# One product per two heads for the token scores of y, one layout for keys and tokens, fewer loads and new order tables in a linear-attention kernel

## The chip, the cores and the metric

The kernel runs on one core of one Trainium2 chip. The metric is device time in microseconds (us), the median of three runs. All data are float32. The engines are named as in the profile: PE (TensorE: matmuls; PEld its weight loads), DVE (VectorE), ACT (ScalarE), POOL (GpSimd) and SP, which only issues the loads and stores (DMAs).

## The reference

There are 4 batches and 8 heads (32 pairs), 768 tokens and 40 channels per head. The first half is a recurrence over tokens in each pair, the second a mixture of experts with soft slots over all 3072 tokens.

```python
for t in range(S):                                   # S = 768, D = 40
    y[t]  = r[t] @ state                             # state: D x D, zero at first
    Sa    = state @ a[t]
    state = state * w[t] - outer(Sa, b[t]) + outer(v[t], k[t])
x = y as 3072 x 320
logits = x @ phi                                     # 32 slots
slots  = softmax(logits over tokens).T @ x
out    = softmax(logits over slots) @ experts(slots) # 8 experts, 320 -> 1024 -> 320
```

## The kernel before, in words

**Stages.** The 768 tokens are cut into 12 stages `st` of 64 tokens, a stage into two halves `q` of 32. Heads stand in three groups `u` of 3, 3 and 2, so that a group is 120, 120 or 80 partitions (head x channel). In a stage the kernel forms running products of `w` (`scan_s`, `scan_c`, two scans on DVE), scales `k` and `b` by them (`scan_k`), spreads `a` into a block-diagonal matrix (`bd_mult`), and forms token-by-token matrices on PE (`lgram`, `gram`, `gram_0`). `kbtok`, `ctok_of`, `y_sd` and `y_ut` are PE transposes with a copy behind each.

**Solves.** Two stages together need the inverse of 1024 small triangular matrices, 32 x 32: the solve `ss` (0 to 5) for the stages 2ss and 2ss+1. `solve_in` transposes the matrices (one 128x1024 transpose on DVE, a copy on ACT), then `solve_step` 1 to 30 run one behind the other, each a multiply and an add over i x (31-i) elements (60 instructions, 30 to 240 elements wide, each needing the one before), then `solve_out` transposes back and `pairs` copies the result into the one buffer `tbs` that the chain reads. Solve 0 has a shorter form (`solve_half`, `solve_join`). A step may stand on DVE or on POOL (`nc.both`); copies may stand on DVE or ACT (`nc.either`).

**Chain.** For each half, `chain_g` gathers what state and earlier tokens give, `chain_u` multiplies by the solved matrices and writes the 32 new u tokens, and `chain_s` forms the state for the next stage. `vu` holds v and u tokens of a stage as 128 rows, `kbks` the k and b tokens in the same order of rows.

**y.** `y_p` forms, for each pair, the 128 x 64 matrix P = (v and u tokens) x (r), masks it into `ppb` on DVE, and `y_y` multiplies P by `kbks` and adds state times r. `vud` holds v and u with channels on partitions, `rds` holds r so: the heads of a pair of heads lie on partitions 0 to 39 and 64 to 103. A y_p call covers 4 heads of all 4 batches: two 32-row halves of tokens x two partition ranges x 8, which is 32 matmuls of 40 rows, 64 columns and 64 moving columns, into two PSUM banks that fill together.

**Slots and experts.** `slots_a` to `slots_e` run for every second stage; from stage 8 on the expert weights (13 MB) are loaded into buffers that stages no longer need. At the end the experts and the output products run.

**Order.** The Python code only records operations. Four tables of numbers set what is built: `ORDER` the sequence of all operations (and so of each engine), `PICK` the engine of each operation that may stand on two, `BANK` the PSUM bank of each, `PACED` the earlier load for which a load waits. An engine runs its operations strictly in its sequence. Every record of the profile has line 1178, the last line that records, so rows are told apart by tile and shape: `ps` is PSUM, `wt` and `mem` are SBUF (numbers after `wt_` differ by buffer, wt_72 is the solve's), `cs_t` the constants.

Of the kernel before, what the change touches and what calls it, by code (L numbers as in the profile page):

```python
# [14 lines left out]
MEM = 9400  # L15

B, H, S, D = 4, 8, 768, 40
# [95 lines left out]
class Engine:  # L113
# [12 lines left out]
    "Cu0203070904100005010F060I0H0G0K0J0E0R0S0A0B0C0V0U0Z0Y0W0X0a0b0h0c0d1d0f0l0e0m0N0L0M0Q1V0O0k0g1a1-1z212O1+2N1j1k"  # L126
    "221b1Z0T0i0j0n0o0s0z0u3N1u3K0t0y0p0q0r081P1X1v1q1r0w1f0+0-1l241m1o1t262511122A2C2Z2a2m2b2c2j13140x1i2B2F1g1h0v1c"
    "151628292o2p2n272G1718191A2R0D2T2P2Q0P1n1s2d2e1B1C2x331p2h1D1E1F1G2-1H1I2f2i3D2+3Z1J1K2H2g4S4v1L1M2y1N1O1Q1R2z36"
    "2E2W1S2X2I2l3738393C2J2K2Y3135346T7C5G5v2D2k322w2v4O4Q4M4q3S3o3T3r3A3V4u3B3E5H5u4Y4d5i5tAj631y1Y1e3P3Q3W3X3Y4E3R"
    "2r2L1T2t232U2u3b3p2V4k2q3F3O303j4-3H3L3a4C3U3q3I3J5U3d3e3f3g3c3k4g204h1U4e2M4j1W4i1w6V3h3i3l3m4D4F4I4G4J4H4P3n3s"  # L130
    "4W4b3t3u4f4X4c3v3w3x3y4R4T3z3+4U4n6i3-4041424344454647485N5I5L494A601x6Z6U6a2s565C4K4L3G3M4N4a4l4r4t5l4V4Z6g5O5P"
    "6K5j714m4p4o4w59585B5A575J5k6A4y516O6P6x6w5D5E5M4s4x4z6S7u4B4+50525354555T6G6N5V5W6W6c5y5X5Y6-705Z5a5b5c5R5r5m5q"
    "5n5p5o5d5e696X7B5f5g6m6n6o6p6H6J6q6r6Q6R6s6t6u6v727D7G7H7I686L6Y7f7z6B6E6I78797765675z64615+666b5-2S8B747A6C6D6F"
    "6l6k6j916d88629B9D999G7U7V5K5S5h5x757E7F7N5s5w7M7Q7d9I7L7c5F5Q6M6y6z7R7b7X7Z7a7S7T7i7t767O7g7w737JA0937K7j7y6h6+"
    "7P7h7v8C8R8-6f8H7x8h7e7l9V7+808182837-847m8T9F8F8f7W7Y8S8g8m7k9E8W8i8j8+8d8Y8D856e8789978A8G86APAT9A9+8a8k8l8E95"
    "949890AD92BQBfB1B6BRBS8b8c8e8z8n8p9CAFBcBdBo8V8ZAHA7AAAcAGAd8U8X8oA19JA5ANBp9H9z9w9x9v9yAMALBOBqC1CAA4ACA2AyB0B5"
    "AIAJDoCUCoDqAEAKAW9-A8A9BHBI7n7o7p7q7r7s8I8J8K8LDtDuEb8M8N8O8P8Q8q8r8sAhAxAm96AO8t8u8v8w8x8y9K9LA3A-9M9N9O9P9Q9R"
    "9S9TAXAaAbAYAZAtAv9U9WABA+Be9X9Y9Z9aEhEoEqGY9b9c9d9e9f9g9h9i9j9kB9BA9l9mA6AV9n9o9p9q9r9s9t9uBlBtBuBsBmAwAzB8EREc"
    "IXB-C0BDBEBPIYJHKnNjBMBUBLASARAiAeAqArAfApAQAoCZB3BKBNBYBZAUCcAkCdAnCaAlEOEPBbBnB4BFAsAuBTBVBWBkBrBgB2B7BhAgBGC+"
    "BiBvB+C3BBBCBJCBCHCGCFCECfC-CCCLC2C7BxByBwC9CzEdBjCICJBXBaC4CvDzCDCTCWCVE0CgCmBzC5DgChD4D2CiD1DnD3DxEKF6CyEGEMEZ"  # L140
    "DrDyD+CKCeE9EBECETEVEWCbE5CYCXE6E1E8E3D-FaFRE+FAEAEFEHE7FcE2FdE4FeFYENEQF7FKELEXD0DpCxD5EIESEUFEEyF1GEDsDvFGEkEn"
    "GzFFFHCwDwEDEEEJEgEuGIEfEtEwExF2EvFJFCFDF8GGGPEYElEsFBEiEjFyFzH4GkGlGvH2F3F4F5EaEmEeEpErC6C8CMCNCOCPCQCRCSCjJ0J8"
    "KACkClCnCpCqCrCsCtFnFxFkFjFhD6D7D8D9DADBDCDDEzF0DEDFDGDHDIDJDKDLF9FIFMFPFQFLFODMDNE-FZFNDODPDQDRJQJRJaJcDSDTDUDV"
    "DWDXDYDZDaDbFUFVDcDdFoG8DeDfDhDiDjDkDlDmG9GMGLGVGNFpF+F-K0JgKgMYG6G7G0G1G4KFKmNVONFwFvGHFWFXFbFlFiFuFtFTFSIHIBGi"
    "GmG2G3GCFsIgFgIhFfIFFmG5GZIzJ6GAGBGJGKGTGUGDGSGaGRFqFrGQITIUJOGFGWH7HAGcGfGgGeGsGoGqGpH3GrINItGnGyG-IvG+H5IxIuGt"
    "GuH6GdGjIKGhGxILIsICIGIJGOGwGXGbHaHBIOIPIQISH+HzIVIWKDIMIaH1H9I-J9JDH8IRJBJEJIJ1J7IZIkIDIfIpIiImIIIqIlIjJkJCJbIc"
    "IwJAIrJtIoJmJiJGInH0J5JTJUIdJ3IyJ4I+J2JMJWJZK4KHKRK-IbIeK1JSJzJyJXK8KqKsJKJNJPJJJVLNJdJhK6K7JeKEJfK2K3KzLKLOJwKM"
    "KJKOKIKPKGK9LULcLdMEMHKZKbKeJLJxJ-JYKNHCHDHEHFHGHHHIHJHKHLMQN9MXHMHNHOHPHQHRHSHTLILYJFJvJsHUHVHWHXHYHZHbHcKKKLHd"
    "HeHfHgHhHiHjHkKtKxKvKyL2L7KwHlHmJ+K5KCHnHoHpHqMxNDNNPiHrHsHtHuHvHwHxHyH-I0KWKlI1I2LRLTI3I4I5I6I7I8I9IAL3L4L9L6L5"
    "LJLXLZNYMINbMZK+LPLSLeLfQ2R8SBSCKTKSKQJjJnJrJqJpJlJuJoKBMgLDL0L8LFLGLHMAMTLxM1L-M3KVKdL1LWKULyLzKaLLLMKXKjKrKuLa"  # L150
    "LhLiM0M6M7M9M8M5M4KYKhMBMSKcKpMLMWMJMKMMLbLgMCKfKkMuMyMjMpLBKiKoLQLVOpMNN8NANBMwMvMPNKNPL+MDNONQNTNJNMNRNSNZMlMk"
    "MrMsMnMqMoMmMtO5O9NHNoNWNXNaLAN-O2O1MhMeLCLEMfMdMbMcM2N7NFNfNLNcNUNdMONCNENlNmPTPUPXNGNINnOGNeNiNpNwOFPbNrNtNvNu"
    "NsOKOOPSPZPdNxOPNqOMPjQ0Q1Q3QINkNyOHNgNhOLLjLkLlLmLnLoLpLqLrLsQOQoR3LtLuLvLwMFMGMRMUOWP3O4O8O0MVMaMzM+M-N0N1N2N3"
    "N4N5N6OZOaObOcOIOVOJOTOSOkOUOROdOeOfOgOhOiPkQEQFQrOjOlOmOnOoOrOsOtOuOvOQPEOwOxOyOzO+O-P0P1P2PLPOPPPgQQQJPDPMPNRC"
    "QHRyRlOYPFPIRKSST1TSODOEP9PAP8OBO6P7OCPmPBP4PGPHIEMiROQcQeQYOXP5PKPYPVPWPfOqP6NzO3N+Q6O7OAPcPtPJPQPaPlPyPzPrPqQG"
    "PpPeQyPvP-PwP+Q4PCPoPsQPQRQ7Q8QWQKQVQNQTQLPRQMQUQ5QDQ+Q-R5QlQnQpQAQbQ9QZQCQBQaQXQdRURNR0R1R9QgQhQjQsR4RARHR7RFRG"
    "QkQmPuQSQvR2QxQqQtRdRLRhRgRjRiRfReQiRIRkR6RJQzRERqRmRuS5SFRDRnRoQuQwRBSOSUSLRbRvS8ThSzSWSjRZS9SERsRwRxS7RaRtSwS6"
    "TFSdSJSKSRSTRRRTS2RSRYRQRPS1RXRcS0TcRrS3R+SDRpSQT9TfSMSPTdQfTXTYPnRMSASHSVSYSXPhPxRzTsR-S4SgSeSlSGSISySNSfSZSbSh"
    "SoSsT0SkSnSiSmTZUMRWUZRVTaUNTbUbTeTgTiTkTzSpSrSuSaScT2TjSqSvSxStS+S-T7T3T4T5T6TtTvU3UYT8TDTETGTITJTATBTHTNTCTOTK"
    "TLTPTQTRTTTUTVTlTmTMTrUBUCUFUHUUUVTWU7U6U4U5U8TnTpTqT+T-UKU9UQURTuTyUAUSUDULTwToTxU0U1UEUIUGUJU2UOUXUWUTUPUaVTVU"  # L160
    "VWUfUgUjUkUlUcUdUeUhUiUmUnUoUpVKUqVBUrUvUyUtUxUwUzU-U+ViV0V4V5UuV1V6V8UsV2V3V9VQVSVRVAVGVbVVVYVLVsVoVpV7VCVFVXVt"
    "VuVwVvVIVOVDVEVJVNVHVMVPVcVaVjVdVeVkVlVZVfVgVhVnVmVqVr"
)
PICK = (
    "1111111011101011111110111110111111111111101110111111111111111011110110000110111100000010111111111111111101110111"
    "1110100111101111111111011111111111111111111111111101100111011111111111111111111011111100111111110000100000111111"
    "0001011111111111101111111111111111111111111111101111111011111011010111001111101111111101111110011001110001000100"
    "0000011111111111111111110111111111111111111111111111101111101101111011110011101111111111111110111111001111111110"
    "0010111111111111111111111111111011111111111111111111111111101111110111101111100111000111001011001001111111101110"
    "0010100001001111111111111111111111111001101011111100101110100101110100111100010010101011011111001111101110110011"  # L170
    "0000001110000"
)
BANK = (
    "0124330665270356725170002715272651376477011662725022576356353677314002527664236431054353014141760614503307542036"
    "4112000525435170332747620055514236215264115760656350364577213000251211745346746053267560420137745611203447604257"
    "7463660534374045170563617055724023305471707031557670623623465312771643617171525354542056247615463136335114020744"
# [1265 lines left out]
```

## Time and profile before

| | us |
|---|---|
| median of 3 runs (404.92 to 413.21) | 405.3 |
| the profiled execution, its own time | 405.49 |
| its span, first to last instruction | 403.7 |
| PE busy | 337.1 |
| DVE busy | 295.4 |
| POOL busy | 199.4 |
| ACT busy | 189.4 |
| 16 DMA engines busy, mean | 56.6% |

The span has four stretches by what runs: the start up to the first transpose of solve 1 (57 us), five solves with the chain of stages 0 to 9 beside them (57 to 307), the last two stages with their y and slots (307 to 357), and experts and output (357 to 404). Busy time of PE includes the modelled way of each matmul through the array, so neighbours overlap. 1.8 us of the profiled time lie outside the span.

### The profile page before, as it was taken

The page shows a single profiled execution, that of the slowest core. Times are in us where ns is not written, and L with a number is a line of the kernel's source. Part 1 is how long each engine was busy: PE and PEld are TensorE (multiplying, and loading weights), DVE is VectorE, ACT ScalarE, POOL GpSimd, SP SyncE. Part 2 cuts the span into 40 slices and gives each one's busy share as a digit, 9 for nine tenths or more (in the row PEclk, how much of TensorE's full clock was granted, in tenths as well). Part 3 has the DMA queues.
Part 4 walks back from the last instruction along what each step waited for, and adds up shares of the span by engine and source line. Part 5 has one row for each costly group of instructions (what it writes and reads, how often), then busy time and mean ns, then how long its engine had stood idle before and what let it go on. Part 6 is the DMA issues. An engine that isn't in the chain of part 4 may idle for free.

```text
span 403.7 us, 18293 instructions
## 1 busy us (share of the span) xinstructions
PE 337.1 (84%) x8097; PEld 295.6 (73%) x8097; DVE 295.4 (73%) x563; ACT 189.4 (47%) x399; POOL 199.4 (49%) x280
## 2 busy tenths in 40 slices
PE   0496689988899798999769998599989899889960
PEld 0386578877798797899569988588888887633960
DVE  7999979688799778998377897478778487651160
ACT  2332546655767456756444763545143514233140
POOL 6933825888167981599824998424860000030000
PEclk9999559999699899999956999999999899989995
DMA  7994804276814734328116577467779667980066
GB/s 186 262 233 113 210 3 97 53 188 147 203 54 107 170 92 120 83 64 229 45 62 145 157 182 237 142 157 232 225 169 248 207 203 208 312 296 13 3 175 215
DMA packets 65966, 63.06 MB, mean 156 GB/s; under 512 B 35857, under 2 KB 53633, under 8 KB 65889
## 3 DMA queue, kind: packets, MB, share of 16 engines
q1 hardware_dynamic: 65889, 61.91, 56.6%
q8 instruction: 63, 1.03, 1.1%
q14 instruction: 14, 0.11, 0.1%
HBM read 57.96 MB, written 3.93 MB: 153 GB/s over the span
## 4 chain that ended last, share of the span: by engine, by line
PE 38%; POOL 31%; DVE 13%; issue 8%; DMA 4%; ACT 2%; SPq 0%; DVEq 0%; POOLq 0%; ACTq 0%
PE ps L1178 38%; POOL wt L1178 31%; DVE wt L1178 11%; DMA wt<-in_kb_dram 3%; ACT wt L1178 1%; DMA wt<-in_ww_dram 1%; ACT mem L1178 1%; DVE ps L1178 1%; DVE mem L1178 1%; DVE mid L1178 0%; SPq L1178 0%; DVE slx L1178 0%; DVE old L1178 0%; ACT mid_r L1178 0%; DMA mem<-in_rd_dram 0%
## 5 line engine op out<-in xcount | busy, mean ns | idle before, releaser
L1178 POOL TENSOR_TENSOR wt<-wt 128x234 f32<-128x234 f32 (+14 forms) x237 | 151.4, 639 | 85.9 <-DVE wt L1178 38.0
L1178 PE MATMUL ps<-wt,wt 120*32 120x96 f32 (+9 forms) x3432 | 149.8, 246 | 32.3 <-POOL wt L1178 17.3
L1178 PEld LDWEIGHTS ps<-wt,wt 120*32 120x32 f32 (+7 forms) x3432 | 134.6, 135 | 42.4 <-POOL wt L1178 17.5
L1178 ACT ACTIVATE wt<-ps 32x320 f32<-32x320 f32 (+1 forms) x129 | 55.4, 429 | 30.5 <-PE ps L1178 28.8
L1178 PE MATMUL ps<-cs_t,wt 120*128 120x120 f32 (+4 forms) x448 | 65.3, 284 | 2.5 <-DVE wt L1178 1.7
L1178 DVE TENSOR_TENSOR wt<-ps,cs_t 128x512 f32<-128x512 f32 (+2 forms) x96 | 56.8, 612 | 10.1 <-PE ps L1178 9.6
L1178 ACT COPY wt<-ps 128x320 f32<-128x320 f32 (+2 forms) x81 | 39.5, 507 | 41.4 <-PE ps L1178 38.3
L1178 PEld LDWEIGHTS ps<-cs_t,wt 120*128 120x128 f32 (+4 forms) x448 | 49.5, 148 | 7.2 <-DVE wt L1178 2.4
L1178 DVE TENSOR_TENSOR_SCAN wt<-wt,wt 120x781 f32<-120x781 f32 (+1 forms) x24 | 46.1, 1926 | 2.2 <-DMA wt<-in_ww_dram 1.6
L1178 PE MATMUL ps<-mem 64*64 64x40 f32 (+2 forms) x648 | 41.1, 253 | 5.0 <-DVE wt L1178 4.0
L1178 PE MATMUL ps<-wt,mem 64*64 64x40 f32 (+3 forms) x1072 | 40.1, 254 | 3.6 <-issue 1.7
L1178 PEld LDWEIGHTS ps<-wt,mem 64*64 64x64 f32 (+3 forms) x1072 | 36.6, 135 | 7.5 <-issue 3.3
L1178 DVE TENSOR_TENSOR wt<-wt 128x108 f32<-128x108 f32 (+19 forms) x91 | 34.3, 377 | 10.0 <-POOL wt L1178 7.6
L1178 POOL TENSOR_TENSOR wt<-wt,wt 120x768 f32<-120x768 f32 x17 | 34.4, 2033 | 9.3 <-DMA wt<-in_aa_dram 4.3
L1178 DVE STREAM_TRANSPOSE wt<-wt 128x1024 f32<-128x1024 f32 x12 | 24.8, 2068 | 18.7 <-POOL wt L1178 17.4
L1178 ACT ACTIVATE wt<-wt,bm_t 120x768 f32<-120x768 f32 (+1 forms) x35 | 29.0, 861 | 12.1 <-POOL wt L1178 4.0
L1178 PEld LDWEIGHTS ps<-mem 64*64 64x64 f32 (+2 forms) x648 | 26.8, 141 | 9.7 <-DVE wt L1178 5.0
L1178 PE MATMUL ps<-mem,wt 40*64 40x64 f32 x1536 | 29.0, 228 | 0.3 <-DVE wt L1178 0.2
L1178 PEld LDWEIGHTS ps<-mem,wt 40*64 40x64 f32 x1536 | 26.4, 142 | 2.7 <-issue 1.2
L1178 ACT COPY mem<-ps 120x480 f32<-120x480 f32 (+4 forms) x45 | 18.1, 408 | 20.6 <-PE ps L1178 11.8
L1178 DVE TENSOR_TENSOR wt<-wt,wt 120x768 f32<-120x768 f32 x20 | 23.8, 1198 | 0.2 <-DMA wt<-in_kb_dram 0.2
L1178 DVE TENSOR_TENSOR ps<-ps,wt 120x480 f32<-120x480 f32 (+1 forms) x30 | 17.8, 602 | 6.7 <-PE ps L1178 6.7
(96 smaller groups left out, 282.5 us busy)
## 6 DMA issues: line engine op xcount, KB each, us to landing
wt<-in_w_dram SPq DMA_DIRECT2D x16, 640.0 KB
wt<-in_kb_dram SPq DMA_DIRECT2D x36, 240.0 KB
wt<-in_w_dram SPq DMA_DIRECT2D x16, 512.0 KB
wt<-in_ww_dram SPq DMA_DIRECT2D x12, 366.6 KB
mem<-in_rr_dram SPq DMA_DIRECT2D x36, 120.0 KB
mem<-in_rd_dram SPq DMA_DIRECT2D x48, 80.0 KB
wt<-in_vv_dram SPq DMA_DIRECT2D x24, 160.0 KB
wt<-in_vd_dram SPq DMA_DIRECT2D x48, 80.0 KB
```

What stands on the lines that cost most here:

```text
L1178: nc.gpsimd.memset(ysb, 0.0)
```

## The change

- **P of y.** `rds` becomes 2048 columns wide, zeroed once, and holds r of the two heads of a pair beside each other in block-diagonal form. One matmul of 104 rows, 128 columns (all 64 v and 64 u tokens) and 128 moving columns gives P of two heads at once: 8 matmuls where 32 stood. Four of them fill a bank, so a call has two banks that fill one after the other; masks and their number stay.
- **Layout.** All 64 v tokens stand ahead of the 64 u tokens, and k ahead of b in the same way (`kb`, `kbks`, `vu`, `vud`, the masks). Instruction counts there stay.
- **Loads.** Per stage v comes in one load instead of two, r and v with channels on partitions in two loads instead of four each (the rows of v now 256 bytes, not 128). For the group of two heads 80 rows are loaded instead of 120 (r from the first stage, k, b and a from stage 5). 321 loads and stores become 261.
- **Buffers.** Two of three `q0s` buffers move into `wt4`; `mem` shrinks by 270 columns. POOL zeroes `rds` once, ahead of everything.
- **Tables.** ORDER, PICK, BANK and PACED are new. Of the 300 solve steps 137 stand on DVE instead of 63, 163 on POOL instead of 237; of the 71 steps of 210, 220, 238 and 240 elements on POOL 27 are left. Of the copies and small multiplications that may stand on DVE, 23 move to ACT or POOL and 8 come.

```diff
-        rds = space(1024)
+        rds = space(2048).rearrange("p (a c) -> p a c", a=2)
...
-        vud = late7[:, 0:2048].rearrange("p (x q c k t) -> p x q c k t", x=2, q=2, k=2, t=32)
+        vud = late7[:, 0:2048].rearrange("p (x c k t) -> p x c k t", x=2, c=8, k=2)
...
         def bdr_at(st):
-            for x in range(2):
-                for p in range(2):
-                    r = slice(64 * p, 64 * p + D)
-                    load(vud[r, x, :, :, 0].rearrange("p q c t -> p (q c) t"), vd[st, p, :, x].rearrange("d (c t) -> d c t", t=32))
-                    load(rds[r, 512 * x:512 * x + 512], rd[st, p, :, x])
+            for p in range(2):
+                r = slice(64 * p, 64 * p + D)
+                load(rds[r, p], rd[st, p].rearrange("d x c -> d (x c)"))
+                load(vud[r, :, :, 0].rearrange("p x c t -> p (x c) t"), vd[st, p].rearrange("d x (c t) -> d (x c) t", t=64))
...
         def vload(st):
             vu = vus.put(st)
-            for q in range(2):
-                load(vu[64 * q:64 * q + 32], vv[st, 32 * q:32 * q + 32])
+            load(vu[0:64], vv[st])
...
         def y_p(st, x):
-            g = [bank(f"ppp{st}"), bank(f"ppq{st}")]
-            nc.gather = True
             for k in range(2):
+                g = bank(f"pp{st}")
                 for b in range(B):
-                    for q in range(2):
-                        for p in range(2):
-                            r = slice(64 * p, 64 * p + D)
-                            c = 64 * (B * k + b)
-                            nc.tensor.matmul(g[p][64 * q:64 * q + 64, c:c + 64],
-                                             vud[r, x, q, B * k + b].rearrange("p k t -> p (k t)"),
-                                             rds[r, 512 * x + c:512 * x + c + 64], start=True, stop=True)
-            nc.gather = False
-            for p in range(2):
+                    c = B * k + b
+                    nc.tensor.matmul(g[:, 128 * b:128 * b + 128], vud[0:104, x, c].rearrange("p k t -> p (k t)"),
+                                     rds[0:104, :, 512 * x + 64 * c:512 * x + 64 * c + 64], start=True, stop=True)
                 t64 = lambda t: t.rearrange("p (g t) -> p g t", t=64)
-                nc.vector.tensor_tensor(t64(ppb.put(4 * st + 2 * x + p)), t64(g[p]),
+                nc.vector.tensor_tensor(t64(ppb.put(4 * st + 2 * x + k)), t64(g),
                                         mask_p.unsqueeze(1).broadcast_to([128, 8, 64]), ALU.mult)
...
 PICK = (
-    "1111111011101011111110111110111111111111101110111111111111111011110110000110111100000010111111111111111101110111"
+    "0101111010011110111111111111111111111100101111111111111111111111111111111100110011001110000011000111001111111111"
```

**On DVE, within solve 3.** The program order of DVE in before, from about the middle of the solve: `wt_72<-wt_72` are solve steps (the shape is i x width), `wt_70<-wt_70,wt_71 120x780` is a scan, `ps_62<-ps_62,wt_76` and `wt_76<-` the state (`chain_s`), `wt_77<-ps` masks of P or gram_0.

```order
L1178 TENSOR_TENSOR wt_72<-wt_72 128x9x22
L1178 MEMSET ones 128x1
L1178 TENSOR_TENSOR wt_72<-wt_72 128x210
L1178 SCALAR_TENSOR_TENSOR wt_70<-wt_70,wt_71 120x780
L1178 TENSOR_TENSOR ps_62<-ps_62,wt_76 120x480
L1178 TENSOR_TENSOR wt_77<-ps_61,cs_t 96x384
L1178 TENSOR_TENSOR wt_76<-ps_62,wt_77 120x480
```

The same place of the same solve on DVE in the changed program:

```order
L1163 TENSOR_TENSOR wt_72<-wt_72 128x220
L1163 RECIPROCAL wt_71<-wt_71 120x12
L1163 TENSOR_TENSOR wt_72<-wt_72 128x11x20
L1163 SCALAR_TENSOR_TENSOR wt_70<-wt_70,wt_71 120x780
L1163 TENSOR_TENSOR wt_72<-wt_72 128x228
L1163 TENSOR_TENSOR wt_77<-ps_66,cs_t 128x512
L1163 TENSOR_TENSOR wt_77<-ps_61,cs_t 128x512
L1163 TENSOR_TENSOR mem<-ps_63,mem 128x128
L1163 TENSOR_TENSOR wt_72<-wt_72 128x12x19
L1163 TENSOR_TENSOR wt_77<-ps_64,cs_t 128x512
```

In before the 210-wide add is the last step of solve 3 on DVE, and the scan and all behind it run while POOL does the other 40 steps; now steps of every width stand between the scan, the masks and the rest.

**On POOL, within solve 3.** POOL's program order in before, from the multiply of step 10 on:

```order
L1178 TENSOR_TENSOR wt_72<-wt_72 128x10x21
L1178 TENSOR_TENSOR wt_72<-wt_72 128x220
L1178 TENSOR_TENSOR wt_72<-wt_72 128x11x20
L1178 TENSOR_TENSOR wt_72<-wt_72 128x228
L1178 TENSOR_TENSOR wt_72<-wt_72 128x12x19
L1178 TENSOR_TENSOR wt_72<-wt_72 128x234
L1178 TENSOR_TENSOR wt_72<-wt_72 128x13x18
```

and in the changed program (`wt_73<-wt_73,wt_70` is the multiplication in `scan_c`, `wt_77<-wt_71,bm_t` a small one in `scan_s`):

```order
L1163 TENSOR_TENSOR wt_72<-wt_72 128x210
L1163 TENSOR_TENSOR wt_72<-wt_72 128x10x21
L1163 TENSOR_TENSOR wt_77<-wt_71,bm_t 120x36
L1163 TENSOR_TENSOR wt_73<-wt_73,wt_70 120x768
L1163 TENSOR_TENSOR wt_72<-wt_72 128x234
L1163 TENSOR_TENSOR wt_72<-wt_72 128x13x18
L1163 TENSOR_TENSOR wt_72<-wt_72 128x17x14
```

Steps 10 to 29 stood in one run on POOL; now POOL has two to seven steps at a time, and other work between them.

**On SP, at the start.** The first loads in before (`b` is b of the first two stages, `ww` is w, `kb` k and b):

```order
L1178 DMA wt_70<-in_ww_dram 120x782
L1178 DMA wt_74<-in_aa_dram 120x768
L1178 DMA wt_76<-in_b_dram 120x768
L1178 DMA wt_74<-in_aa_dram 120x768
L1178 DMA mem<-in_b_dram 120x768
L1178 DMA wt_70<-in_kb_dram 120x512 x4
```

and in the changed program:

```order
L1163 DMA wt_70<-in_ww_dram 120x782 x2
L1163 DMA wt_74<-in_aa_dram 120x768
L1163 DMA wt_70<-in_kb_dram 120x512
L1163 DMA wt_73<-in_aa_dram 120x256
L1163 DMA mem<-in_b_dram 120x768
L1163 DMA bm_t<-in_consts_dram 120x3
L1163 DMA wt_74<-in_aa_dram 120x768
L1163 DMA cs_t<-in_consts_dram 128x32
L1163 DMA wt_76<-in_b_dram 120x768
```

b of stage 0 (`wt_76`) was the seventh load and is now the tenth, behind a part of k that stage 1 needs and a part of a that stage 2 needs.

## Rows read from the trace of the kernel before

**Rows 1.** Page, part 1: busy us (share of the span) xinstructions.

```profile
PE 337.1 (84%) x8097; PEld 295.6 (73%) x8097; DVE 295.4 (73%) x563; ACT 189.4 (47%) x399; POOL 199.4 (49%) x280
```

**Rows 2.** Windows: from:to, length, busy PE PEld DVE ACT POOL, PEclk, DMA, GB/s.

```profile
0.00:57.00 57.00, 32.97 (x881) 29.38 (x882) 50.42 (x70) 21.44 (x36) 33.65 (x23) 0.84 0.71 178
57.00:105.00 48.00, 42.85 (x1137) 38.80 (x1136) 39.36 (x68) 29.06 (x58) 33.53 (x48) 0.96 0.51 117
105.00:157.00 52.00, 48.21 (x1178) 45.04 (x1178) 42.64 (x68) 31.46 (x64) 33.69 (x50) 0.92 0.44 114
157.00:206.00 49.00, 41.59 (x1044) 37.40 (x1040) 38.91 (x70) 28.93 (x61) 34.14 (x49) 0.96 0.39 105
206.00:262.00 56.00, 50.39 (x1191) 46.21 (x1191) 41.96 (x74) 30.76 (x66) 38.26 (x57) 0.87 0.62 167
262.00:307.00 45.00, 43.27 (x1153) 38.55 (x1150) 35.11 (x77) 18.26 (x43) 22.74 (x47) 0.98 0.73 205
307.00:357.40 50.40, 46.17 (x1125) 38.79 (x1121) 35.24 (x97) 18.04 (x48) 1.01 (x4) 0.97 0.80 238
```

**Rows 3.** Chain in order of time: start, us, what (solve 2, three of its steps).

```profile
130.40 1.98 POOL wt L1178
...
139.36 0.68 POOL wt L1178
140.10 0.60 POOL wt L1178
```

**Rows 4.** Groups by shape on POOL: xcount | busy us, mean ns | idle before.

```profile
L1178 POOL TENSOR_TENSOR wt<-wt 128x238 f32<-128x238 f32 x19 | 19.1, 1004 | 2.4 <-DVE wt L1178 1.0
L1178 POOL TENSOR_TENSOR wt<-wt 128x240 f32<-128x240 f32 x19 | 18.3, 963 | 1.5
...
L1178 POOL TENSOR_TENSOR wt<-wt 128x210 f32<-128x210 f32 x16 | 14.5, 904 | 6.3 <-DVE wt L1178 5.3
L1178 POOL TENSOR_TENSOR wt<-wt 128x220 f32<-128x220 f32 x17 | 13.8, 813 | 4.6 <-DVE wt L1178 3.4
...
L1178 POOL TENSOR_TENSOR wt<-wt 128x130 f32<-128x130 f32 x13 | 5.9, 455 | 4.5 <-DVE wt L1178 3.8
```

**Rows 5.** Groups by shape on DVE, 57 to 307 us: solve steps.

```profile
L1178 DVE TENSOR_TENSOR wt<-wt 128x130 f32<-128x130 f32 x7 | 2.1, 295 | 1.5 <-POOL wt L1178 1.2
...
L1178 DVE TENSOR_TENSOR wt<-wt 128x240 f32<-128x240 f32 x1 | 0.4, 408 | 1.6 <-POOL wt L1178 1.6
```

**Rows 6.** Groups on DVE, whole span: closing and opening transposes of solves; copies from PSUM.

```profile
L1178 DVE STREAM_TRANSPOSE wt<-wt 128x1024 f32<-128x1024 f32 x12 | 24.8, 2068 | 18.7 <-POOL wt L1178 17.4
...
L1178 DVE COPY wt<-ps 128x320 f32<-128x320 f32 (+2 forms) x27 | 13.1, 515 | 9.0 <-PE ps L1178 8.2 <-ACT mem L1178 0.8
```

**Rows 7.** Timeline of POOL and of DVE, 129 to 145 us: start, us, engine, operation, xcount.

```profile
128.92 8.85 POOL L1178 TENSOR_TENSOR wt<-wt 128x240 f32<-128x240 f32 x7
...
130.01 1.95 DVE L1178 TENSOR_TENSOR_SCAN wt<-wt,wt 120x780 f32<-120x780 f32 x1
...
137.95 7.30 POOL L1178 TENSOR_TENSOR wt<-wt 128x234 f32<-128x234 f32 x10
```

**Rows 8.** Waits of DVE, 57 to 307 us: us in total, times, longest.

```profile
DVE wt L1178 <- POOL wt L1178: 25.3, 14, 6.9
```

**Rows 9.** Timeline of PE: start, us, operation (rows x columns, moving), xrecords.

```profile
171.06 1.16 PE L1178 MATMUL ps<-mem,wt 40*64 40x64 f32 x64
172.04 0.67 PE L1178 MATMUL ps<-mem 64*64 64x40 f32 x17
...
224.95 0.65 PE L1178 MATMUL ps<-cs_t,wt 128*104 128x128 f32 x4
225.43 0.73 PE L1178 MATMUL ps<-wt,wt 128*80 128x80 f32 x8
226.00 0.74 PE L1178 MATMUL ps<-cs_t,wt 80*128 80x80 f32 x6
```

**Rows 10.** Chain in order of time at the start.

```profile
6.06 10.20 DMA wt<-in_kb_dram
```

## What the change will do to the time

> **What bounds the kernel now.** I read the busy shares first, then the windows by stretch, then the groups by shape, the chain and the waits. Over the whole span no engine is full: PE 84%, DVE 73% [rows 1]. The windows say more [rows 2]. In the five stretches from one solve's opening transpose to the next (57 to 307 us, 250 us in all) PE is busy 42.85 + 48.21 + 41.59 + 50.39 + 43.27 = 226.3 us (91%) and DVE 39.36 + 42.64 + 38.91 + 41.96 + 35.11 = 198.0 us (79%), while POOL is busy about 162 us, most of it solve steps. So three things run near their ends at once: PE's work, DVE's work, and the serial chain of 60 steps in each solve, to whose end the next two stages are tied. In the tail (307 to 357) PE alone is near full, 46.17 of 50.4 us.
>
> What do the steps cost? A step of 234 elements on POOL takes 0.60 to 0.68 us, and steps start 0.74 us apart (139.36 to 140.10) [rows 3]; ten of them fill 7.30 us [rows 7]. Just before, seven steps of the widest forms needed 8.85 us, and one of them 1.98 us: it began at 130.40, and DVE had begun a scan of 1.95 us at 130.01 [rows 3, 7]. So a POOL step is stretched while DVE runs an operation from SBUF to SBUF. In the mean the 71 widest steps on POOL are busy 19.1 + 18.3 + 14.5 + 13.8 = 65.7 us [rows 4]; at the clean 0.60 each they would take 42.6. About 23 us are stretching. DVE itself does a step of 240 elements in 0.41 us and one of 130 in 0.30 [rows 5], against 0.60 and 0.455 on POOL [rows 3, 4].
>
> DVE is idle 250 − 198 = 52 us of the loops. Of that 25.3 us are waits on POOL [rows 8], and over the whole span 17.4 us of such waits stand before the transposes of the solves [rows 6], that is, DVE had nothing else left and waited for the end of a solve. Without them 27 us remain, nearly all behind PE.
>
> **The change part by part.** *Solve steps.* 74 steps go from POOL to DVE, 44 of them of the four widest forms (71 on POOL become 27). On the chain a wide one gains 0.60 − 0.41 = 0.19 us, plus up to 0.05 for the shorter gap between steps: 44 x 0.24 = 10.6. The other 30 gain 0.455 − 0.295 = 0.16 each: 4.8. The engine changes 74 more times within the solves (42 to 116); a hand-over is not shown apart, and I bound it between 0 and the 0.07 between two POOL steps, taking half: −2.6. The chain is 12.8 us shorter. Then the 27 wide steps left on POOL carry 27/71 of the stretching, 8.8 us instead of 23: another 14.3. If the chain alone set the time, the loops would go from 250 to **223** us.
>
> DVE pays for it: 44 x 0.41 + 30 x 0.30 = 27 us more. 23 copies and small operations leave it and 8 come, 15 net at 0.5 us [rows 6] = −7.5. Six more operations run ahead of solve 1's opening transpose than before (75 for 69), which takes some 5 us out of the loops and into the start. DVE in the loops: 198 + 27 − 7.5 − 5 = **213 us**. That is 95% of 223, so the chain cannot have all of its gain. DVE is in strict order: in before the last steps of solve 3 on POOL ran with nothing of the solve queued on DVE, and a mask that waited for PE delayed no step. Now steps of every width stand behind scans, masks and copies, so each wait of DVE for PE becomes a wait of the chain. I take the loops from DVE: 213 us busy, the 27 us behind PE as they are, and waits on POOL of 5 us (before, 25.3 − 17.4 = 7.9 outside the transposes, taken lower because POOL's runs become shorter). The wait before the transposes goes, since DVE now does part of the late steps itself. Sum 245, **−5 us**. The bounds: 223 (−27, the chain alone) and DVE at its present 79%, 213/0.79 = 270 (+20).
>
> *P of y.* The tiled product is 64 records, and the next group starts 172.04 − 171.06 = 0.98 us after it [rows 9]. The new one is 8 matmuls of 128 columns, by the two records per matmul of before (64 for 32) 16 records. Eight records of 80 columns are followed after 226.00 − 225.43 = 0.57 us, 0.071 each, so 0.114 for 128 columns; four transposing records of 128 columns after 225.43 − 224.95 = 0.48, 0.12 each [rows 9]. So 16 x 0.114 = 1.83 us: **0.85 us more** each, 0.94 by the other row. There are 24, of which 20 fall in the loops: PE 226.3 + 17 = 243 of 250 us. It lies beside the solves and costs nothing there as long as PE has a pause elsewhere; with the loops at 245 that is 99% of PE, and a part of the pauses now spent behind DVE must close. The other four fall in the tail: 3.4 us on an engine that is busy 46.17 of 50.4 us. About half can be hidden in its 4.2 us of pauses: **+1.5** (0 to +3.4). The two PSUM banks now fill one after the other, so the first mask can start 0.9 us earlier; nothing waits there that long. Masks and their number stay.
>
> The Trainium skill (TensorEngine Tiling (Array Packing), Theoretical Speedup) speaks against this part: where dimensions are at most 64, tiles are said to give up to 2 times per dimension. By it the full array would take as much as four times as long, 3.9 us for 0.98, +70 us of PE over 24. The rows agree in sign but not in size, since block-diagonal r puts two heads through each pass; they give 1.9 times.
>
> *Start.* b of stage 0 moves from seventh load to tenth, and DVE has six more operations ahead of solve 1. In before, k and b are the transfer waited for at the start (6.06, 10.20 us) [rows 10], and DVE is busy 50.42 of 57 us [rows 2], so 5 us of added DVE work have 6.6 us of pauses to go into. A part will not fit: **+1.5** (0 to +5).
>
> *Loads.* 60 fewer loads and stores, behind a DMA that is not a bound (16 engines busy 39 to 80% in the windows of rows 2): **−0.5** at most. The new order of rows in `vu`, `kbks` and the masks moves no instruction and costs nothing; zeroing `rds` stands on POOL ahead of everything, under the first loads.
>
> *Sum.* Against the profiled time of 405.5 us, 0.2 above the median: −5 + 1.5 + 1.5 − 0.5 = −2.5, **403.0 us**.
>
> **The rivals.** *R1, faster: DVE fills its pauses.* If the searched order also puts each mask behind the PE work that it needs, the 27 us behind PE shrink and the loops go towards the chain's 223. For it: in 105 to 157 DVE already reached 82%. Against it: 95% on an engine that takes from PE, ACT, POOL and DMA. Midway, at 234 (DVE at 91%): 405.5 − 16 + 2.5 = **392**. It needs 89% of DVE or more to pass the 2% bound (loops under 239).
>
> *R2, slower: DVE's waits grow with its share of the chain.* DVE keeps the share of idle time it has, since a wait for PE now holds up the chain too. At its best share of today, 82%, 213 takes 260 (+10): **418**; at 79% 428. It decides below 83.4%, where the loops pass 255 and the time 413.4. For it: DVE is at 75 to 82% in all five stretches, though their other loads differ. Against it: half of today's idle time was behind POOL, and has lost its cause.
>
> *R3, slower: PE becomes the bound.* 243 us of PE work in the loops; its stretches reach 85 to 96% today. At 94.5%, between 93 and the best 96, the loops take 257 (+7): **415**. For it: 17 us come and none go. Against it: busy time is modelled and overlaps.
>
> *R4: the tiled product costs its neighbours too.* If each one emptied the array before and after, dropping 24 would give time back. The row bounds it: 16 rounds of four tiles at 0.057 (64 columns at the 0.071 for 80) are 0.91 of the 0.98, so at most 0.07 per product inside and, granting as much again on both sides, 0.2: 24 x 0.2 = 5 us of PE, about **398**, if PE is what holds. A rule of the Trainium skill on the same page (Key Properties: a change of tiling mode drains the TensorE) says that such a cost exists; no row of before shows more than this.
>
> **How the numbers follow.** The likeliest case 0.40, R1 0.29, R2 0.15, R3 0.12, R4 0.04. The first alone would range from 397 to 413, since its bounds are those of DVE's share between 83.4 and 89%. Faster by over 2% (under 397.2) is R1, and the lower half of R4 and of the first case gives it 0.04 more: 0.33. Slower (over 413.4) is R2 and R3: 0.27. The rest, 0.40, is within 2%, which is about what a measurement of this kernel can tell from no change. For 8 in 10 the range takes R1 down to 390 and R2 and R3 up to 419.
>
> **What would show it.** Right, if DVE's share in the loops lies at 84 to 89%, the loops near 49 us each, no wait on POOL over 2 us before the transposes, most wide steps at 0.41 us on DVE, and the ones left on POOL nearer 0.65 than 0.9. The new product must show 16 records and about 1.8 us to the next group; solve 1's opening transpose comes at 57 to 60 us; the tail takes 52. R1 shows as DVE over 89%, R2 as many DVE waits for PE with POOL idle behind DVE, R3 as PE over 94% in each stretch with DVE waiting for it. Wrong altogether it would be if the granted clock fell for longer than now (0.87 to 0.98 in the loops [rows 2]), since PE has no room for it.

## The result and the profile after

The changed kernel takes 388.6 us in the median (385.6 to 392.4, four runs) against 406.4 of the kernel before in the same rounds: a ratio of 0.955 (95% interval 0.946 to 0.964). Forecast were 403.0 us, 390 to 419, with "faster" at 0.33. The direction was that of the first rival (392), and the median lies 1.4 us under the range. Executions of one kernel differ by up to 4% here, the slower ones mostly at a lower mean clock, and the ratios and their intervals are of the fast ones alone.

The busy times of the page (part 1), and windows of the trace, cut where before was cut: the start up to solve 1's opening transpose, five stretches from one opening transpose to the next (the last ends with solve 5's closing one), tail, experts. The columns are those of rows 2.

```profile
PE 338.2 (88%) x6945; PEld 300.5 (78%) x6945; DVE 298.0 (78%) x622; ACT 192.0 (50%) x408; POOL 145.1 (38%) x213
```

```profile
0.00:60.11 60.11, 36.23 (x950) 32.68 (x951) 49.19 (x75) 26.41 (x50) 25.68 (x23) 0.80 0.68 180
60.11:102.82 42.71, 41.46 (x928) 38.94 (x926) 39.48 (x77) 24.15 (x48) 21.66 (x34) 1.00 0.39 93
102.82:150.03 47.21, 46.49 (x1000) 43.63 (x998) 43.15 (x78) 30.54 (x64) 25.77 (x38) 1.00 0.55 117
150.03:198.08 48.05, 47.15 (x1007) 43.84 (x1005) 44.45 (x88) 34.28 (x75) 25.52 (x37) 1.00 0.55 136
198.08:245.59 47.51, 47.09 (x1031) 44.10 (x1032) 42.10 (x88) 29.59 (x61) 23.61 (x35) 1.00 0.60 147
245.59:287.46 41.87, 40.66 (x799) 37.29 (x799) 34.59 (x82) 18.12 (x41) 19.45 (x42) 1.00 0.82 234
287.46:338.00 50.54, 46.68 (x849) 38.68 (x844) 34.12 (x97) 18.48 (x48) 3.40 (x6) 0.97 0.84 239
338.00:383.80 45.80, 32.42 (x408) 21.34 (x408) 10.93 (x41) 10.39 (x26) 0.00 (x0) 0.80 0.44 127
```

Beside rows 2: the start is 3.1 us longer, the tail and the experts are the same to half a microsecond, and all of the gain is in the loops, 227.4 us for 250. There PE is busy 222.9 us, 98%, at a granted clock of 1.00 in every stretch, where rows 2 showed 0.87 to 0.98. DVE is busy 203.8 us, 90%; POOL's busy time falls from 162 to 116. On the chain of work that ended last (page, part 4) PE's share rises from 38 to 67% of the span, and POOL's falls from 31 to 4%.

Solve steps by shape on POOL, and one on DVE (groups as in rows 4 and 5):

```profile
L1163 POOL TENSOR_TENSOR wt<-wt 128x220 f32<-128x220 f32 x10 | 9.3, 934 | 9.7 <-DVE wt L1163 9.4
...
L1163 POOL TENSOR_TENSOR wt<-wt 128x210 f32<-128x210 f32 x8 | 6.1, 760 | 3.0 <-DVE wt L1163 2.7
L1163 POOL TENSOR_TENSOR wt<-wt 128x238 f32<-128x238 f32 x5 | 5.3, 1060 | 8.0 <-DVE wt L1163 7.9
L1163 POOL TENSOR_TENSOR wt<-wt 128x240 f32<-128x240 f32 x4 | 3.9, 984 | 6.2 <-DVE wt L1163 6.2
```

```profile
L1163 DVE TENSOR_TENSOR wt<-wt 128x240 f32<-128x240 f32 x16 | 6.5, 406 | 1.1 <-POOL wt L1163 0.7
```

All steps on POOL together, before and after, and DVE's transposes of the solves after (groups of the pages, the second answering to rows 6):

```profile
L1178 POOL TENSOR_TENSOR wt<-wt 128x234 f32<-128x234 f32 (+14 forms) x237 | 151.4, 639 | 85.9 <-DVE wt L1178 38.0 <-ACT wt L1178 31.6
```

```profile
L1163 POOL TENSOR_TENSOR wt<-wt 128x30 f32<-128x30 f32 (+14 forms) x163 | 99.5, 610 | 101.8 <-DVE wt L1163 84.3
...
L1163 DVE STREAM_TRANSPOSE wt<-wt 128x1024 f32<-128x1024 f32 x12 | 25.7, 2139 | 1.2 <-POOL wt L1163 0.4
```

DVE's waits in the loops (us in total, times, longest; rows 8 of before), three of the rows:

```profile
DVE wt L1163 <- PE ps L1163: 6.4, 13, 1.2
DVE wt L1163 <- POOL wt L1163: 4.9, 11, 0.8
DVE ps L1163 <- PE ps L1163: 4.6, 7, 1.3
```

A step left on POOL is stretched as much as before, 0.76 to 1.06 us for the four widest forms (0.81 to 1.00 before), but there are 27 of them for 71. The wait for the end of a solve is gone: 0.4 us before the transposes for 17.4 [rows 6]. No wait of DVE is longer than 1.3 us.

### The profile page after: what moved, and what is told of

Same layout as the page of the kernel before. It is cut to its first block, busy times and chain, and to the rows that moved or that the text cites. A ratio compares the mean times of both kernels' runs of the same rounds, so it can differ in the third digit from the quotient of the medians.

```text
span 383.8 us, 15934 instructions
## 1 busy us (share of the span) xinstructions
PE 338.2 (88%) x6945; PEld 300.5 (78%) x6945; DVE 298.0 (78%) x622; ACT 192.0 (50%) x408; POOL 145.1 (38%) x213
## 4 chain that ended last, share of the span: by engine, by line
PE 67%; ACT 9%; DVE 8%; issue 5%; POOL 4%; DMA 3%; SPq 1%; DVEq 0%; ACTq 0%; POOLq 0%
PE ps L1163 67%; DVE wt L1163 7%; ACT wt L1163 7%; POOL wt L1163 4%; DMA mem<-in_b_dram 2%; ACT mem L1163 1%; SPq L1163 1%; DMA mem<-in_vq_dram 1%; DVE mid L1163 0%; ACT L1163 0%; ACT mid L1163 0%; DVE ps L1163 0%; DVE mem L1163 0%; DMA wt<-in_kb_dram 0%; ACT old L1163 0%
## 5 line engine op out<-in xcount | busy, mean ns | idle before, releaser
L1163 PE MATMUL ps<-wt,wt 96*32 96x40 f32 (+9 forms) x3432 | 138.9, 237 | 18.7 <-ACT wt L1163 16.6
L1163 PEld LDWEIGHTS ps<-wt,wt 120*32 120x32 f32 (+7 forms) x3432 | 126.0, 128 | 25.2 <-issue 17.6
L1163 POOL TENSOR_TENSOR wt<-wt 128x30 f32<-128x30 f32 (+14 forms) x163 | 99.5, 610 | 101.8 <-DVE wt L1163 84.3
L1163 DVE TENSOR_TENSOR wt<-ps,cs_t 128x512 f32<-128x512 f32 (+2 forms) x104 | 62.0, 618 | 7.2 <-PE ps L1163 6.3
L1163 ACT COPY wt<-ps 128x320 f32<-128x320 f32 (+2 forms) x87 | 41.7, 503 | 39.5 <-PE ps L1163 31.7
L1163 DVE TENSOR_TENSOR wt<-wt 128x234 f32<-128x234 f32 (+18 forms) x165 | 54.1, 328 | 9.3 <-POOL wt L1163 4.5
L1163 PE MATMUL ps<-mem,wt 104*128 104x128 f32 (+1 forms) x640 | 57.8, 258 | 0.3 <-DMA mem<-in_rd_dram 0.2
L1163 PEld LDWEIGHTS ps<-mem,wt 104*128 104x128 f32 (+1 forms) x640 | 53.3, 169 | 2.1 <-issue 0.6
L1163 POOL TENSOR_TENSOR wt<-wt,wt 120x768 f32<-120x768 f32 x17 | 29.8, 1770 | 26.0 <-DMA wt<-in_kb_dram 19.4
L1163 ACT COPY mem<-ps 120x480 f32<-120x480 f32 (+4 forms) x52 | 21.1, 419 | 27.6 <-PE ps L1163 26.4
L1163 PE MATMUL ps<-mem 120*64 120x120 f32 (+2 forms) x392 | 30.3, 259 | 0.0
L1163 DVE STREAM_TRANSPOSE wt<-wt 128x1024 f32<-128x1024 f32 x12 | 25.7, 2139 | 1.2 <-POOL wt L1163 0.4
L1163 ACT COPY wt<-wt 120x768 f32<-120x768 f32 (+3 forms) x19 | 16.2, 856 | 12.6 <-DVE wt L1163 11.1
```

The costliest lines, as they stand in the source:

```text
L1163: nc.vector.memset(one_f, 0.0)
```

## The experiments

The theories: A, the split of the steps shortened the chain until PE was left as the bound; B, the searched order did it, or DVE or the chain still holds the loops; C, part of the gain is the granted clock; D, the new product or the fewer loads did it. Each run has the kernel before timed beside it; a ratio is to that, and stands where the record has one. In the texts on record, A and B are the theories of that one run. Loops are again solve 1's opening transpose to solve 5's closing one: 250.3 us before, 227.4 after.

**The code under the old tables.** The changed code, with ORDER, PICK, BANK and PACED of before:

```
 ORDER = (
-    "6n0005060A011L0L0P0H0J0C020G07030B0D0E0h0R0F0T0V0b0i0p0n0f0j0N0a0e0g0l1i0u0x0v0r0O0K0Q0I0M0814180k0Y090Z0U0d0X0z"
+    "Ce0304080A0511000106020G070J0I0H0L0K0F0S0T0B0C0D0W0V0a0Z0X0Y0b0c0i0d0e1c0g0m0f0n0O0M0N0R1V0P0l0h1Z1+1y1-2M1z2L1i"
...
```

> The changed code (product of 104 rows, new layout, 261 loads) under the tables of the kernel before: old order, old engines of all steps and copies, old banks; merged loads stand where they fit beside the old ones. Theory A (the code costs PE 0.85 us per product and brings nothing by itself, since the chain of the solves holds the old order): 405 to 420 us against 405 to 416 of the kernel before on this chip. Theory D (the product or the fewer loads are what brought the gain): under 396 us.

424.1 us, ratio 1.034 (1.017 to 1.050). The loops in a window, and PE's longest waits in them:

```profile
57.36:315.91 258.55, 235.84 (x4709) 216.78 (x4709) 197.86 (x353) 137.47 (x288) 163.15 (x251) 0.95 0.53 131
```

```profile
PE ps L1169 <- DMA mem<-in_rd_dram: 10.8, 4, 5.1
```

D falls: the code without its tables costs time. PE's busy time grows by 9.5 us. But 10.8 us are waits for the merged loads of r, which land too late in this order, so the run does not price the product alone. Taken off, they would leave some 413 us, an estimate, which is still no gain.

**The split in the old order.** The kernel before, with only the characters of PICK that belong to solve steps as in the changed one (160 of 300 steps change engine, 117 of them to DVE and 43 to POOL; the 74 of the prediction is the difference):

```
 PICK = (
...
-    "1111111011101011111110111110111111111111101110111111111111111011110110000110111100000010111111111111111101110111"
+    "1111111011101011111110111110111111111111101110111111111111111011111111111110110011001010000011000111001101110111"
...
```

> The kernel before with one thing changed: each solve step stands on the engine that it has in the changed kernel (137 on DVE, 163 on POOL), in the old order. Theory A (the shorter chain of the solves brought the gain, and the order only makes room for it): most of the gain is here, 388 to 394 us. Theory B (the searched order of everything else brought it; the steps now stand behind masks and copies that wait for PE): 400 to 412 us.

485.3 us, ratio 1.185 (1.167 to 1.204): the longest of all. The profile is of the longest of its four executions, 493.9 us; the shortest took 481.2. One of three pauses of PE of about 20 us, and DVE at the same time (timelines):

```profile
142.59 1.13 PE L1178 MATMUL ps<-mem,wt 40*64 40x64 f32 x62
162.57 1.67 PE L1178 MATMUL ps<-wt,wt 120*96 120x96 f32 x9 [18.84 <-POOL wt L1178]
```

```profile
148.28 2.23 DVE L1178 TENSOR_TENSOR wt<-wt 128x238 f32<-128x238 f32 x5 [1.51 <-POOL wt L1178]
152.71 0.38 DVE L1178 TENSOR_TENSOR wt<-wt 128x210 f32<-128x210 f32 x1 [2.20 <-POOL wt L1178]
...
161.47 0.95 DVE L1178 TENSOR_TENSOR wt<-wt,wt 120x768 f32<-120x768 f32 x1
162.34 0.69 DVE L1178 TENSOR_TENSOR wt<-ps,cs_t 128x512 f32<-128x512 f32 x1
```

From 142 to 161 us DVE runs nothing but solve steps and waits for POOL's steps between them. The scaling of k and the mask of P, for which PE waits, stand behind the last step in DVE's order. (The row names POOL, whose own last step ends at the same time, 162.5.) The same split that the changed kernel has is ruinous where the steps stand next to each other: a wait for POOL on DVE then holds up everything, and there are 80.6 us of them:

```profile
DVE wt L1178 <- POOL wt L1178: 80.6, 52, 5.1
```

Theory A, as I stated it, falls.

**The old split in the new order.** The changed kernel with the steps' engines of before, by the same edit the other way:

```
 PICK = (
...
-    "0101111010011110111111111111111111111100101111111111111111111111111111111100110011001110000011000111001111111111"
+    "0101111010011110111111111111111111111100101111111111111111111111110110000100111100000110111111111111111111111111"
...
```

> The changed kernel with one thing undone: each solve step stands on the engine that it had in the kernel before (63 on DVE, 237 on POOL), in the new order. Theory A (the split of the steps): the chains grow by 13 us and the stretching on POOL returns, 400 to 410 us. Theory B (the order of the rest): at most 393 us.

424.9 us, ratio 1.040 (1.030 to 1.050): 36 us over the changed kernel. Loops, and DVE's waits in them:

```profile
61.34:326.55 265.21, 240.64 (x4759) 223.56 (x4759) 181.50 (x337) 137.69 (x285) 155.88 (x259) 0.92 0.49 124
```

```profile
DVE wt L1163 <- POOL wt L1163: 31.7, 14, 5.2
DVE wt L1163 <- PE ps L1163: 30.3, 24, 4.8
```

Here PE's work is that of the changed kernel, and still PE is busy 240.6 us for 222.9: about 41 of the 265 us ran at half clock (a mean of 0.92), and none of the changed kernel's loops did.

So B in its plain form falls too. The fair comparison is with the other run of the new code under the old split: with the old order that took a ratio of 1.034, with the new order it takes 1.040, so the new order alone gains nothing. DVE has 22 us less to do than in the changed kernel and still waits 31.7 us for POOL, and 42.1 us for PE over all rows. Split and order bring the gain only together. The new code with the new split in the old order was not run; that case is shown on the old code alone, by the run ahead of this one.

**Dummy matmuls in PE's pauses of before** (a table that is empty in both kernels):

```
 FILLS = (
-    ""
+    "7RBFAB9BG+PFJuH7"
```

> The kernel before with dummy matmuls of 128 columns (11, 9, 25 and 17 of them) ahead of the four operations at which PE pauses for 2.8, 2.3, 6.3 and 4.2 us (99.9, 134.4, 198.7 and 256.0 us) and after which the granted clock falls to half for 7, 3, 17 and 3 us. Theory C (part of the gain of the change is the clock: without the pauses PE keeps 2.4 GHz): the 30 us at half clock go, worth up to 15 us of PE's work: 392 to 398 us. Against it (what PE does at half clock there is hidden behind the solve's chain, or the clock falls for another reason): 403 to 408 us.

418.5 us, ratio 1.022 (1.010 to 1.035): no gain, but the run is half a test. The first place did what it should. PE in before, and here (windows):

```profile
103.40:110.20 6.80, 6.80 (x78) 6.45 (x68) 5.49 (x5) 5.37 (x12) 0.00 (x0) 0.50 0.84 208
```

```profile
102.00:110.00 8.00, 7.37 (x220) 6.80 (x212) 7.98 (x9) 7.15 (x15) 0.99 (x4) 1.00 0.99 224
```

With the pause filled, the fall of the clock behind it is gone. At the second place PE paused for 1.0 and 0.5 us ahead of the dummies, and the clock fell all the same. The last two groups waited themselves, as it seems for the PSUM bank in which I had put them (line 379 is theirs):

```profile
PE ps L379 <- DVE wt L1178: 5.8, 1, 5.8
PE ps L379 <- ACT wt L1178: 3.5, 1, 3.5
```

so they filled nothing and came on top. In all, the loops ran about 33 us at half clock, as many as before (windows of half a microsecond). That pauses and clock belong together is shown at one place; what the clock alone is worth in this kernel stays open.

**The tiled product in the new order.** P as it was formed before, in 10 stages, then in the three (3, 8, 10) where nothing else has to move:

```
+            for c in range(2 * B):
+                for q in range(2):
+                    for p in range(2):
+                        r = slice(64 * p, 64 * p + D)
+                        nc.tensor.matmul(gs[p][64 * q:64 * q + 64, 64 * c:64 * c + 64],
+                                         vud[r, x, c].rearrange("p k t -> p (k t)")[:, 64 * q:64 * q + 64],
+                                         rds[r, p, 512 * x + 64 * c:512 * x + 64 * c + 64], start=True, stop=True)
```

> The changed kernel with P of y formed by the old tiled product (32 matmuls of 40 rows, 64 tokens, 64 columns) in 10 of the 12 stages; everything else as changed, but seven products y_y stand a few places later and three loads behind them. The trace of the changed kernel shows PE busy 222.9 of 227.4 us between the first transposes of solve 1 and the end of solve 5. Theory A (PE is the bound now): 20 products give back 0.85 to 0.9 us each, 17 to 18 us of PE, about 14 of them in the loops: 370 to 377 us. Theory B (DVE, busy 203.8 of 227.4 there, takes over nearly at once): the loops cannot go under about 220, and the time is 381 to 386.

> The changed kernel with P formed by the old tiled product in stages 3, 8 and 10 only, where no other operation has to move for it. 6 products give back 0.85 to 0.9 us of PE, 5.2 us. Theory A (PE is the bound): 380 to 384 us against 385.6 to 389. Theory B (another bound, or the merged product makes its two banks wait for each other, as in the run with ten stages): 386 to 393.

413.9 us (407.2 to 421.1; the kernel before took 414.4 beside it) and 400.5 us (395.3 to 402.8; ratio 0.977, 0.967 to 0.987): both slower than the changed kernel, though PE has less to do, and both over the ranges of both their theories. In the first, other operations had moved as well. In the second nothing had. Solve 5 there took 51.9 us where it had taken 41.9, at a mean clock of 0.80, in a profile of an execution of 402.7 us; the shortest took 395.3 and has no profile. The longer of two pauses in it (timeline of PE; the other is 257.2 to 259.3), the windows of the pause and behind it, and the DMA queues within the pause:

```profile
290.55 0.38 PE L1182 MATMUL ps<-wt,wt 128*64 128x40 f32 x7
293.72 0.22 PE L1182 MATMUL ps<-wt,wt 128*64 128x40 f32 x1 [2.79 <-issue]
```

```profile
285.00:293.00 8.00, 5.47 (x164) 4.46 (x164) 5.64 (x14) 4.19 (x11) 3.63 (x6) 1.00 0.97 211
293.00:300.00 7.00, 6.28 (x46) 5.48 (x46) 1.63 (x4) 0.00 (x0) 2.42 (x5) 0.52 0.56 174
```

```profile
q8 instruction: 1, 0.02, 2.2%
```

PE stops in the middle of a product and waits for nothing that the profile knows ("issue"), while one block of 16 KB on the instruction queue is fetched; then the clock is at half. In before PE stops in the same way from 134.6 to 136.7 us, with a fetch from 134.0 to 135.3. Of the 17 such pauses of 0.4 us or more in the traces of before and after, 16 end 1.2 to 1.7 us after the end of a fetch; most of the 117 fetches there stop nothing. The tiled product spends 64 records where the other spends 16, and PE's program is 6945 records long after for 8097 before. In the whole span PE's pauses of this kind are 14.4 us before, 5.6 after and 13.2 here; in the loops alone 4.2 before and 1.1 after. That fits, but part of the 12 us is a start that was 6 us longer in this profile, where no tiled product runs, so the price of the records stays open.

**What bounds the changed kernel?** Six runs on its own order. It was timed again as the base; in the others work was left out or doubled and every instruction kept its place, only two matmuls of each four went in one of them, and eight stood for four in another.

```
-  nc.tensor.matmul(g[:, 128 * b:128 * b + 128], vud[0:104, x, c]...
+  w = slice(0, 2 if st < 3 else 1)
+  nc.tensor.matmul(g[:, 128 * b:128 * b + 64 * w.stop], vud[0:104, x, c]...
...
+  n = 8 if st < 3 else 4
-  nc.vector.tensor_tensor(t64(ppb.put(4 * st + 2 * x + k)), t64(g),
+  nc.vector.tensor_tensor(t64(ppb.put(4 * st + 2 * x + k))[:, 0:n], t64(g)[:, 0:n],
...
-  for b in range(B):
+  for b in range(B if st < 3 else 2):
...
-  tv = tmp_r[i % 2][:, 0:i * m].rearrange("p (j t) -> p j t", j=i)
+  h = (i + 1) // 2
+  tv = tmp_r[i % 2][:, 0:h * m].rearrange("p (j t) -> p j t", j=h)
...
+  for _ in range(2):
       nc.tensor.matmul(g[:, 128 * b:128 * b + 128], vud[0:104, x, c]...
```

These are, in order, half of the moving columns, half of each mask, two of four matmuls, half of each step, and the product twice.

> The changed kernel, unchanged, on the chip and in the rounds of the next three, as their base. Every theory: 385 to 392 us, PE busy 97 to 98% of the loops (from the opening transpose of solve 1 to the end of solve 5).

> The changed kernel with half of the new product left out from stage 3 on (64 of 128 moving columns; P of every second head is stale, so y is wrong there). The order and every other instruction stay. 18 products lose 0.9 us of PE each, 14 of them in the loops. Theory A (PE is the bound at 98% of the loops): the loops get 10 to 13 us shorter, all of it 371 to 377 us against 385.6 to 389. Theory B (DVE or the chain of the solves holds it just as tightly): at most 4 us, 381 to 388.

> The changed kernel with half of each mask of P left out from stage 3 on (256 of 512 elements on DVE; P of two of four batches stays stale, so y is wrong there). The order and every other instruction stay. 36 masks lose about 0.27 us of DVE each, 28 of them in the loops: 7.5 us of DVE there. Theory A (PE is the bound): 384 to 389, no change. Theory B (DVE, 90% busy in the loops, is the bound since its waits are fixed): 377 to 382.

> The changed kernel with two of the four matmuls of each half of y_p left out from stage 3 on (two of four batches keep a stale P, so y is wrong there). The run with 64 of 128 moving columns had left PE as busy as before (8 records still took 0.89 us), so it did not tell the bound; leaving out whole matmuls does take PE time: 0.45 us for each of 36 halves, 28 of them in the loops. Theory A (PE is the bound at 98% of the loops): 12 us less there, 371 to 378 us in all. Theory B (the chain of the solves holds it just as tightly): 382 to 389.

> The changed kernel with each solve step over half of its rows (the inverse is incomplete, so y is wrong). Order and all counts stay; the 300 steps in the loops, 147 us of work one behind the other, become some 95 us, and DVE loses about 15 us. Theory A (PE is the bound at 98% of the loops, the chain no longer): 382 to 388 us, the loops at least 221 us long. Theory B (the chain still sets the loops, with PE just fitting in): the loops fall under 212, all under 375.

> The changed kernel with each matmul of y_p issued twice into the same place. It adds 1.8 us of PE to each of 24 products, 44 us in all, 36 of them in the loops. Theory A (PE is the bound): all of it arrives, 425 to 435 us. Theory B (the loops have room beside PE): 395 to 415.

The base took 391.3 us, ratio 0.944 (0.932 to 0.955). Half the columns 389.4 (383.6 to 392.4); half the masks 386.9, 0.950 (0.940 to 0.960); half the matmuls 385.6, 0.939 (0.926 to 0.951); half the steps 389.8, 0.948 (0.941 to 0.955); twice the product 428.2, 1.043 (1.036 to 1.051). Their loops, in this order from the base on:

```profile
61.86:288.75 226.89, 221.90 (x4729) 206.80 (x4726) 203.75 (x411) 136.80 (x285) 115.71 (x185) 1.00 0.58 145
```

```profile
62.32:290.30 227.98, 223.22 (x4751) 208.71 (x4750) 203.69 (x411) 137.01 (x285) 114.96 (x185) 0.99 0.57 144
```

```profile
61.87:292.10 230.23, 224.03 (x4747) 209.18 (x4744) 198.00 (x411) 136.83 (x285) 115.48 (x185) 0.99 0.56 142
```

```profile
61.18:285.16 223.98, 213.98 (x4625) 195.63 (x4625) 203.15 (x411) 136.50 (x285) 116.15 (x185) 1.00 0.59 147
```

```profile
60.88:289.39 228.51, 222.80 (x4748) 207.71 (x4748) 191.01 (x411) 136.44 (x285) 90.73 (x185) 1.00 0.57 144
```

```profile
59.96:323.77 263.81, 258.02 (x5067) 243.31 (x5067) 205.74 (x411) 136.57 (x285) 113.05 (x185) 1.00 0.50 125
```

Read length and PE first. With the steps halved POOL loses 25 us and DVE 13, and the loops are 1.6 us longer: the chain no longer holds the loops. Masks halved: DVE loses 6, no gain. PE's work raised by 36.1 us: the loops grow by 36.9, all of it. PE's work lowered by 7.9 (with half of the matmuls, less than the 12 expected): the loops shrink by 2.9 only, and PE now waits for others:

```profile
PE ps L1163 <- DVE wt L1163: 4.2, 11, 0.8
```

So PE is the bound of the changed kernel, and DVE with its order stands some 3 us behind it. By its time, 385.6 us, the run with half of the matmuls falls in the range of its theory B; but the chain that B names is not what holds it, as the halved steps show. The run with half of the columns tells nothing on the bound, since PE was as busy as before, but it prices the product; see the last section.

## Why the prediction was wrong

Against the profiled time the terms were: loops −5, start +1.5, tail +1.5, loads −0.5. They came out as loops −22.7, start +3.1, tail +0.1, experts −0.5: the miss is in the loops.

- **Solve steps, the chain: right in size.** Forecast were −12.8 for the moved steps and −14.3 for the stretching, 27 us. POOL's steps lost 151.4 − 99.5 = 51.9 us and DVE's gained 21.7 (25.7 to 47.4 us, summed over the 63 and the 137 steps in the loops): 30 us less in the chain. The 27 wide steps left on POOL are busy 24.6 us, 8.4 over the clean 0.60 each, for the 8.8 of the sum; the sign "nearer 0.65 than 0.9" was at odds with that sum from the start. That the loops of 227 lie near the 223 that stood as the chain's end of the bounds is luck, since with the steps halved they do not shrink.
- **DVE's busy time: 213 forecast, 203.8 measured.** The moved steps cost 21.7 for 27, and scans' multiplications and copies that left the loops took away some 16 for 12.5.
- **The step that failed: "I take the loops from DVE: 213 us busy, the 27 us behind PE as they are".** The loops came out 17.6 us under the 245 of that sum: 9.2 us are DVE's busy time, and 8.3 are its idle time. DVE's waits for POOL were as forecast (4.9 for 5), but its other idle time did not stay: 227.4 − 203.8 − 4.9 = 18.7 us for 27. Its waits for PE fell from 21.1 to 13.1 us over all rows, and most of that is the masks', 8.9 us before and 3.7 after (groups on DVE in the loops, and one row of its waits before):

```profile
L1178 DVE TENSOR_TENSOR wt<-ps,cs_t 128x512 f32<-128x512 f32 x44 | 29.4, 681 | 5.5 <-PE ps L1178 5.4 <-issue 0.2
...
L1178 DVE TENSOR_TENSOR mem<-ps,cs_t 128x512 f32<-128x512 f32 x10 | 6.8, 680 | 3.5 <-PE ps L1178 3.5
```

```profile
L1163 DVE TENSOR_TENSOR wt<-ps,cs_t 128x512 f32<-128x512 f32 x55 | 36.7, 682 | 3.9 <-PE ps L1163 3.7
```

```profile
DVE wt L1178 <- PE ps L1178: 10.4, 12, 2.6
```

  I had argued that in strict order each wait for PE becomes a wait of the chain. The run with the split in the old order shows how dear waits handed on in this way become, 485 us, though there it is DVE that waits for POOL and PE that waits for DVE; split and order together avoid it. The order alone does not: with the old split in it DVE waits 42.1 us for PE. And DVE was not what the loops should have been taken from, since PE is what now sets them; there the forecast had a size wrong too:
- **PE: 243 us of work forecast, 222.9 measured.** With 243 us the loops could not have come to 227. The product cost what was said: 16 records from 164.39 to the next group at 166.18 are 1.79 us, so +0.81 for +0.85.

```profile
164.39 1.95 PE L1163 MATMUL ps<-mem,wt 104*128 104x128 f32 x16
166.18 0.44 PE L1163 MATMUL ps<-cs_t,wt 80*80 80x80 f32 x4
```

  What was wrong is the 226.3 to which it was added. Of the 250 us before, about 33 ran at half clock (four falls of 31 us in all, and the end of the start's; a mean of 0.93), and PE was busy in 30 of them, so some 15 us of that busy time were the clock's: 15 of the 20 us by which the sum was off. The other 5 are not taken apart. The four falls followed pauses of PE of 2.5, 2.1, 6.0 and 4.0 us, three of them waits for the late end of a solve and the second one beside a fetch of code. With split and order changed PE's waits in the loops fall from 22.6 to 3.7 us, it runs at 2.4 GHz throughout, and the work that looked as if it needed 97% of 250 us fits into 223. The run of the old split in the new order has the same work, the pauses and the falls, and PE is busy 17.8 us longer in it; no run changes the clock alone. The prediction warned that it would be wrong altogether if the clock fell for longer; I never asked what it would give if the falls went away.
- **R1** had the right side and a price of 392, since it had DVE at 91% (measured 90%) but 213 us to do. That it comes so near is in part luck: the 243 us of PE's work, which I forecast as well, do not fit into its loops of 234. **R2** does not show in the changed kernel; the split without its order is slower still, and there by waits for POOL (80.6 us). **R3** named the engine that is now the bound, at 98% where I took 96% as the best, and its sign, over 94% in each stretch, is there; it had the wrong side, by the same 243. **R4** does not show: with the tiled product back the time rises.
- **Start:** +3.1 for +1.5, inside its bounds, but by luck: the 5 us of added DVE work are not there (49.2 us busy for 50.4); DVE's waits for PE rose, from 2.3 to 6.8 us. **Tail:** the four products' 3.3 us were hidden, at +0.1. **Loads:** nothing that shows.

## What to carry to other kernels

Where a chain, an engine in strict order and the matmul engine are all near 80 to 90%, do not add a change's work to today's busy time: first take out of it half of what was busy at half clock, and ask whether the pauses before each fall go away. A split of a chain over two engines and the order of everything else on them are one change: here the split without the order made the kernel 19% slower and the order without the split gained nothing, so neither can be priced alone. To find the bound of a kernel that is balanced, double one engine's work and halve the others', and leave every instruction in its place.

## What the runs showed of the hardware

- **A product with 64 moving columns takes as long as one with 128.** With 128 columns of weights, 16 records with half of the moving columns need 1.84 us to the next group here, against 1.79 above:

```profile
262.45 2.00 PE L1164 MATMUL ps<-mem,wt 104*128 104x64 f32 x16
264.29 0.94 PE L1164 MATMUL ps<-cs_t,mid 128*128 128x128 f32 x7
```

  That is 0.112 to 0.115 us a record, with 128 or 64 columns moving. The Trainium skill (TensorE: Matmul & The Clock Gate, LDWEIGHTS (loading the stationary operand)) gives a weight load the time of its columns divided by 1.2 per ns, whatever its rows: 107 ns for 128. The trace agrees to within 8 ns. So a full-width product is paid by its weights here. For the old tiles, four loads of 64 columns at once would make 16 rounds of 53 ns by that rule of the Trainium skill, an estimate of 0.85 us for the measured 0.98; no run here takes them apart.
- **PE stops beside fetches of its code.** Pauses of up to 3.1 us without any wait that the profile knows end 1.2 to 1.7 us after the end of a 16 KB block on the instruction queue, 16 of 17 in before and after. Three in the loops of over 2 us (134.6 in before, 257.2 and 290.9 in the run with three tiled stages) have the half clock behind them. That PE waited for the code is the plain reading of these times; no run takes a fetch away. A form with fewer records keeps PE's program shorter; how much that gave here stays open.
- **A hand-over between POOL and DVE is cheap where nothing stands between** and dear where anything does: with the same engine for each step, DVE's waits for POOL are 4.9 us in the new order (and code) and 80.6 us in the old.
